# Local and global attention ahead of a gated feed-forward: the global queries of four heads put into one tile

## The chip, the cores and the metric

The program runs on one core of one Trainium2 chip. The metric is the device time of one execution in microseconds. For the kernel before the change three runs gave 1267.98, 1266.98 and 1265.59 us, so the median is 1266.98 us.

## What is computed

Each of 8 batches has 8 heads of dimension 64, with 512 local and 32 global tokens. A local query sees the 32 global keys and the local keys at most 32 positions away. A global query sees all 32 + 512 keys. The attention's result, 4608 tokens of 512 numbers, goes through a gated feed-forward with a hidden dimension of 1536.

```
s_g   = scale * q_g @ k_all.T           # 32 queries, 544 keys
out_g = sm(s_g) @ v_all
s_ll  = where(|i - j| <= 32, scale * q_l @ k_l.T, -1e9)
s_lg  = scale * q_l @ k_g.T
out_l = sm([s_lg, s_ll]) @ [v_g, v_l]
x     = [out_g, out_l]                  # per batch, heads side by side
y     = (sigmoid(x @ w_gate) * (x @ w_val)) @ w_out
```

The three weight matrices come as float64 and are turned into two float32r parts (high and low) on the chip; a product is then made of three matmuls, high x high, low x high and high x low.

## The kernel before

**The stream that sets the clock.** The feed-forward is one stream of TensorE matmuls (`ffn_stream`, L347). Its unit is an item: one chunk of tokens and one of 12 blocks of 128 hidden columns. An item has 12 matmuls into `bank_g`, 12 into `bank_v` (both L362) and 12 into `bank_o` (L396). After every four matmuls of 512 columns the generator yields. That is one tick, and a full chunk of 512 tokens has 9 x 12 = 108 ticks. The kernel keeps a list of events, each with a tick and an order; at every yield the driver issues the events that are due. So all work of the attention, of all engines, is written into the gaps between groups of feed-forward matmuls.

**Chunks.** Chunk 0 holds local blocks 0 and 1 of the first batch, chunk 1 its blocks 2 and 3 and its global queries, chunks 2 to 8 a batch each with its 32 global queries. The attention of chunk 0 runs ahead of the stream. The attention of chunk 1 and of chunk 2 runs during the feed-forward of chunks 0 and 1, while the weights are converted as well (`convert`, L119: four DVE operations, one ACT and one POOL operation for a block, three blocks every 4 ticks). From chunk 3 on the attention of one chunk runs in the 108 ticks of the chunk before it, the steady stage: six such periods of 8 heads. The last chunk and then the 256 global tokens of all batches go through the feed-forward with no attention beside them.

**Units of a head.** A head of a full chunk has two local units (two blocks of 128 queries each, `local_unit`, L216) and one global unit (32 queries, `global_unit`, L287). Each unit is a generator of four stages:

- local: (1) scores, four matmuls of 224 columns (L225), then mask and maximum on DVE (L237) and the exponential on ACT (L240); (2) normalisation on DVE (L243, L244 and L213); (3) four transposes of 128x128 on TensorE (L254), split into two float32r parts on ACT (L263) and DVE (L264); (4) four matmuls with the values (L280, L281), summed on ACT, DVE and POOL (L283 to L285).
- global: (1) four matmuls of 256 columns for the local keys (L299) and two of 32 columns for the global keys (L301), each into a PSUM bank of its own, then maxima on DVE (L304 to L306) and two exponentials on ACT (L308, L309); (2) normalisation of `pg`, 32 x 576, on DVE (L311, L312, L213); (3) five transposes of 32 rows (L317), split on ACT (L323) and DVE (L324); (4) five matmuls with the values (L330), summed on ACT, DVE and POOL (L335 to L337).

The heads of chunks 0 and 1 and the first four of chunk 2 use plain float32 ("native" in the code), the others the two float32r parts.

**What sets the order.** In the steady stage the units of a chunk follow each other every `PER` = 4 ticks and their stages lie at 0, 3, 6 and 9 ticks (`STAGES`), so a head takes 12 ticks and the TensorE work of scores, values and transposes falls into three different gaps of every four. `HOLE` puts all events of a chunk from its tick 8 on off by one tick. All PSUM tiles of the attention and `bank_g` and `bank_v` rotate through four buffers of one tag ("att"). The values of a head are in `vhl`, of which there are two buffers.

## Time and profile before

| | |
|---|---|
| median of three runs | 1266.98 us |
| the profiled execution: span from the first to the last instruction (the profile has no other time for it) | 1265.6 us |
| mean granted TensorE clock | 0.986 |
| TensorE matmul busy | 1221.5 us, 97%, 6820 instructions |
| DVE busy | 877.6 us, 69%, 2433 instructions |
| ACT busy | 783.3 us, 62%, 1899 instructions |
| POOL busy | 570.6 us, 45%, 573 instructions |
| bytes moved | 151.90 MB, mean 120 GB/s |
| start of the stream's first matmul | 49.71 us |
| a steady period (feed-forward of a chunk and attention of the next) | 139.1 us |
| the last chunk's feed-forward, with no attention beside it | 100.4 us |

How to read it: engine busy times are from the profile's first part; a busy TensorE is not one at its peak, since matmuls are pipelined and the duration of one includes the time to its last result. What a matmul costs the stream is therefore the distance from its start to the start of the next one, which the timeline gives.

### The profile page before, as it was taken

How to read it: one execution, taken by the hardware profiler on the slowest of the kernel's cores; microseconds unless marked ns; L12 is line 12 of the kernel's file. 1: busy time of each engine (PE TensorE's matmuls, PEld its weight loads, DVE VectorE, ACT ScalarE, POOL GpSimd, SP SyncE). 2: the span in 40 equal slices, each digit the busy share in tenths (PEclk: the TensorE clock that was granted, in tenths of full speed). 3: DMA queues.
4: the chain of work that ended last, by engine and by line, in shares of the span. 5: the costliest groups of instructions: out<-in, count | busy, mean ns of one | idle time of the engine just before them, and what ended most of it. 6: DMA issues, size and time to landing. Idle time of an engine off the chain costs nothing.

```text
span 1265.6 us, 20474 instructions
## 1 busy us (share of the span) xinstructions
PE 1221.5 (97%) x6820; PEld 994.1 (79%) x6820; DVE 877.6 (69%) x2433; ACT 783.3 (62%) x1899; POOL 570.6 (45%) x573
## 2 busy tenths in 40 slices
PE   5899989999999999999999999999999999999998
PEld 4676768788788877888788877888788877888897
DVE  4797976757877777857876778767775787632232
ACT  4586766756666666666666667756765766532233
POOL 1444554545555355545555455535554555311111
PEclk9698999999999999999999999999999999999999
DMA  5576864333333333333333423343334332122143
GB/s 198 197 259 225 254 191 145 92 121 99 92 107 98 115 99 108 91 121 108 107 92 107 126 78 107 109 127 111 92 86 126 116 92 87 44 90 67 67 133 117
DMA packets 59497, 151.90 MB, mean 120 GB/s; under 512 B 6144, under 2 KB 19456, under 8 KB 59392
## 3 DMA queue, kind: packets, MB, share of 16 engines
q1 hardware_dynamic: 59392, 150.59, 38.9%
q8 instruction: 54, 0.88, 0.3%
q14 instruction: 51, 0.42, 0.1%
HBM read 135.36 MB, written 15.20 MB: 119 GB/s over the span
## 4 chain that ended last, share of the span: by engine, by line
PE 77%; DVE 13%; ACT 5%; issue 3%; POOL 1%; DMA 1%; SPq 0%; POOLq 0%; DVEq 0%; ACTq 0%
PE bank_g L362 20%; PE bank_v L362 19%; PE bank_o L396 19%; PE bank_x L225 5%; PE bank_y L254 4%; DVE p_buf L213 3%; DVE th L378 2%; PE bank_y L317 2%; PE bank_x L330 2%; PE bank_x L280 2%; PE bank_x L299 2%; PE bank_x L281 1%; DVE pg_buf L213 1%; ACT s_sb L240 1%; DVE pt L264 1%
## 5 line engine op out<-in xcount | busy, mean ns | idle before, releaser
L362 PE MATMUL bank_g<-xt,wg 128*128 128x512 f32 (+1 forms) x1440 | 340.3, 371 | 1.8 <-DVE th L380 1.8
L362 PE MATMUL bank_v<-xt,wv 128*128 128x512 f32 (+1 forms) x1440 | 332.6, 368 | 3.0 <-DVE pt L264 2.7
L396 PE MATMUL bank_o<-wo,hh 128*128 128x512 f32 x1224 | 334.0, 404 | 0.8 <-ACT hh L382 0.4
L362 PEld LDWEIGHTS bank_g<-xt,wg 128*128 128x128 f32 x1440 | 238.6, 192 | 41.6 <-issue 3.4
L362 PEld LDWEIGHTS bank_v<-xt,wv 128*128 128x128 f32 x1440 | 237.8, 190 | 40.7 <-PE bank_y L301 3.1
L396 PEld LDWEIGHTS bank_o<-wo,hh 128*128 128x128 f32 x1224 | 214.1, 189 | 38.9 <-ACT hh L382 1.2
L383 POOL TENSOR_TENSOR hh<-th,hh 128x512 fp32r<-128x512 f32 (+1 forms) x120 | 137.6, 1147 | 199.7 <-ACT hh L382 198.8
L240 ACT ACTIVATE s_sb<-s_sb,nm 128x224 f32<-128x224 f32 x240 | 113.8, 475 | 143.1 <-DVE nm L237 142.0
L213 DVE TENSOR_SCALAR p_buf<-s_sb,r 128x128 f32<-128x128 f32 (+1 forms) x443 | 151.8, 386 | 4.2 <-PE bank_y L254 0.4
L375 DVE TENSOR_SCALAR mn<-bank_g 128x512 f32<-128x512 f32 (+1 forms) x108 | 67.3, 623 | 110.7 <-ACT th L370 109.3
L378 DVE SCALAR_TENSOR_TENSOR th<-th,mn 128x512 f32<-128x512 f32 (+1 forms) x120 | 101.5, 846 | 59.0 <-ACT mn L376 52.7
L285 POOL TENSOR_TENSOR x<-t 64x256 f32<-64x256 f32 x104 | 76.4, 734 | 142.8 <-DVE t L284 138.7
L194 POOL TENSOR_TENSOR kl<-qk_raw,qk_hi 128x704 fp32r<-128x704 f32 x52 | 88.4, 1701 | 114.8 <-ACT qk_hi L193 114.8
L370 ACT ACTIVATE th<-bank_g 128x512 f32<-128x512 f32 (+1 forms) x120 | 63.5, 529 | 97.7 <-PE bank_g L362 96.1
L382 ACT CAST hh<-th 128x512 fp32r<-128x512 f32 (+1 forms) x120 | 66.5, 554 | 68.1 <-DVE th L380 67.3
L237 DVE CUSTOM_DVE_ANT_0 s_sb<-bank_x,masks 128x224 f32<-128x224 f32 x240 | 83.8, 381 | 12.7 <-PE bank_x L225 8.4
L254 PE MATMUL bank_y<-ident,p_buf 128*128 128x128 f32 x496 | 80.1, 282 | 10.8 <-DVE p_buf L213 6.6
L196 POOL TENSOR_TENSOR qk_hi<-qk_raw,qk_hi 64x256 fp32r<-64x256 f32 x104 | 87.7, 863 | 4.1
L254 PEld LDWEIGHTS bank_y<-ident,p_buf 128*128 128x128 f32 x496 | 60.9, 143 | 32.5 <-ACT pg_buf L308 6.6
L243 DVE TENSOR_SCALAR r<-sm 128x2 f32<-128x2 f32 x128 | 29.3, 229 | 75.5 <-ACT s_sb L240 74.2
L193 ACT CAST qk_hi<-qk_raw 128x1248 fp32r<-128x1248 f32 x52 | 64.1, 1233 | 22.2 <-PE bank_y L301 22.1
L380 DVE TENSOR_TENSOR th<-bank_v,th 128x512 f32<-128x512 f32 (+1 forms) x120 | 72.4, 604 | 5.1 <-PE bank_v L362 1.3
(109 smaller groups left out, 1985.9 us busy)
## 6 DMA issues: line engine op xcount, KB each, us to landing
wo<-wo_dram SPq DMA_DIRECT2D x116, 512.0 KB, 3.5
qk_raw<-in_qk_dram SPq DMA_DIRECT2D x104, 312.0 KB, 4.4
v_raw<-in_v_dram SPq DMA_DIRECT2D x52, 256.0 KB, 2.6
out_dram<-ob SPq DMA_DIRECT2D x34, 256.0 KB, 3.0
xt<-in_w_gate_dram SPq DMA_DIRECT2D x12, 512.0 KB, 4.5
xt<-in_w_val_dram SPq DMA_DIRECT2D x12, 512.0 KB, 4.4
xt<-in_w_out_dram SPq DMA_DIRECT2D x12, 512.0 KB, 4.9
v_nat<-in_v_dram SPq DMA_DIRECT2D x8, 512.0 KB, 5.5
```

The source lines that it names most:

```text
L194: nc.gpsimd.tensor_tensor(kl, t[:, K0:Q1], hi[:, K0:Q1].bitcast(F32), op=ALU.subtract)
L196: nc.gpsimd.tensor_tensor(hi[64:128, r], t[64:128, r], hi[64:128, r].bitcast(F32), op=ALU.subtract)
L213: nc.vector.tensor_scalar(out, in_, by, None, op0=ALU.mult)
L237: anchor[0] = nc.vector.tensor_tensor_reduce(out=s_sb[:, i], in0=s_ps[:, i, 0:WIN], in1=masks[:, m], scale=-0.125, scalar=3.0e38, op0=ALU. ...
L240: nc.scalar.activation(s_sb[:, i], s_sb[:, i], AF.Exp, bias=nm[:, i:i + 1], scale=-1.0, accum_out=sm[:, i:i + 1])
L254: nc.tensor.transpose(pt_ps[:, 2 * i + t], pb[:, i, t * P:(t + 1) * P], ident)
L285: nc.gpsimd.tensor_tensor(dst, t0[:, :, 0], t0[:, :, 1], op=ALU.add)
L362: nc.tensor.matmul(acc, w[a][:, t, fs], xt[:, c, t, x0:x0 + ntok], start=n == 0, stop=n == 11)
L378: nc.vector.scalar_tensor_tensor(th, th, 1.0, mn, op0=ALU.add, op1=ALU.mult)
L380: nc.vector.tensor_tensor(th, acc, th, op=ALU.mult)
L383: nc.gpsimd.tensor_tensor(hh[:, 1, 0:ntok], th, hh[:, 0, 0:ntok].bitcast(F32), op=ALU.subtract)
L396: nc.tensor.matmul(o_ps[t], ph[:, a, t * P:(t + 1) * P], pwo[:, c], start=f2 == 0 and i == 0, stop=f2 == NF - 1 and i == 2)
```

## The change

The rows of four heads' global queries are collected in one tile of 128 partitions. `pg` grows from 32 to 128 partitions; head h writes its scores, unscaled, into partitions 32 (h mod 4) and up. Softmax, transposes and their split are then made once for four heads, by the last of them; the matmuls with the values are made for all four heads in one stage, 5 for each as before. The scores with the 32 global keys are no longer a matmul pair into a bank of their own: the second local unit of the head computes them ahead of its own scores, in columns 224 to 255 of the first block of its score bank, of which local scores use 224, and ACT copies them to `pg`. In `pg` these 32 keys now stand in columns 96 to 127, ahead of the 512 local ones, and the value rows on the host get a copy of the global values to match.

The schedule: a head takes `TICKS` = 12.25 ticks in place of 12, with its two local units 6.125 ticks apart (in place of 4, with the global unit in the third place). A local unit's transposes lie 6.125 ticks after its scores (in place of 6), which is the tick of the next unit's scores; at equal ticks the transposes come first. The global scores lie in the tick of the first unit's last stage, the other global stages 4, 6.75 and 11 ticks later. The first unit of a chunk starts at tick 1 in place of 3. For chunk 1 a head takes 2.2 ticks as before (one local unit, a global unit with offsets of its own), for chunk 2 it takes 9 as before; since the stages scale with the gap between local units, chunk 0's units (4 ticks apart as before) have stages at 0, 1.96, 4 and 5.88 ticks in place of 0, 3, 6 and 9.

Five value buffers in place of two, because the values of four heads are needed at once. `dynamic_dma_scratch_size=512` is passed to the program's constructor and frees the memory that they take.

```diff
-BASE, PER = 3, 4
-STAGES = (0, 3, 6, 9)
+GH = P // SG
+G0 = P - SG
+VBUFS = GH + 1
+BASE, TICKS = 1, 12.25
+LOCAL = ((0, 3), (3, 2), (TICKS / 2, 2), (9, 2))
+GLOBAL = ((9 - TICKS / 2, 3), (13 - TICKS / 2, 2), (15.75 - TICKS / 2, 2), (20 - TICKS / 2, 2))
+GLOBAL_HALF = ((2, 3), (4, 2), (6, 2), (10, 2))
-START = dict(per0=4, base1=1, per1=1.1, base2=23, per2=3, x2=28, lead=8, native_heads=4)
+START = dict(per0=4, base1=1, per1=2.2, base2=23, per2=9, x2=28, lead=8, native_heads=4)
...
-    pg = const.tile([32, 5 * P], F32, name="pg_buf")
+    pg = const.tile([P, 5 * P], F32, name="pg_buf")
...
         s_ps = ps.tile([P, 2, 256], F32, name="bank_x", tag="att", bufs=4)
+        with_gg = T["with_g"] and blocks[-1] == 3
+        if with_gg:
+            gg = s_ps[0:SG, 0, WIN:]
+            for t, (kt, k0) in enumerate(zip(ks, k0s)):
+                nc.tensor.matmul(gg, ks[0][:, QK - SG - q0:QK - q0], kt[:, k0 + 96:k0 + 128],
+                                 start=t == 0, stop=t == last)
...
+        if with_gg:
+            nc.scalar.copy(pg[SG * (h % GH):SG * (h % GH + 1), G0:P], gg)
         yield
...
-        for t, (src, k0) in enumerate(zip(ks, k0s)):
-            nc.tensor.matmul(sb, qg, src[:, k0 + 96:k0 + 128], start=t == 0, stop=t == last)
...
+        nc.scalar.copy(pg[SG * (h % GH):SG * (h % GH + 1), P:], sa)
+        if h % GH < GH - 1:
+            return
+        keys = pg[:, G0:]
+        nc.vector.tensor_reduce(mg[:, 0:1], keys, axis=AX.X, op=ALU.max)
+        nc.vector.tensor_scalar(mg[:, 0:1], mg[:, 0:1], -0.125, None, op0=ALU.mult)
+        nc.scalar.activation(keys, keys, AF.Exp, bias=mg[:, 0:1], scale=0.125, accum_out=sg)
         yield
+        nc.vector.tensor_scalar_add(mg[:, 1:2], sg, 1e-9)
+        nc.vector.reciprocal(mg[:, 1:2], mg[:, 1:2])
+        scaled(0, keys, keys, mg[:, 1:2])
         yield
+        for bank, c0, c1 in (("bank_x", 1, 5), ("bank_y", 0, 1)):
+            pt_ps = ps.tile([P, c1 - c0, P], F32, name=bank, tag="att", bufs=4)
+            for c in range(c0, c1):
+                nc.tensor.transpose(pt_ps[:, c - c0], pg[:, c * P:(c + 1) * P], ident)
+            nc.scalar.copy(pt[:, c0:c1, 0:P], pt_ps)
+            if not nat:
+                nc.vector.tensor_tensor(pt[:, c0:c1, P:], pt_ps, pt[:, c0:c1, 0:P].bitcast(F32), op=ALU.subtract)
         yield
+        o_ps = ps.tile([64, GH, 32] if nat else [P, GH, 2, 32], F32, name="bank_x", tag="att", bufs=4)
+        for g in range(GH):
+            vt = heads[h - GH + 1 + g]["v"]
+            for i, c in enumerate((1, 2, 3, 4, 0)):
+                p_c = pt[:, c].rearrange("p (a g q) -> p a g q", g=GH, q=SG)[:, :, g]
+                nc.tensor.matmul(o_ps[:, g], vt[:, (VS[3:] + VM)[c], :], p_c, start=i == 0, stop=i == 4)
...
-            for i in range(npu):
-                t0 = base + per * i
-                for o in STAGES:
-                    ev.append((t0 + sc * o, 2, lambda h=h, i=i: adv(h, i)))
+            for i in range(nu + with_g):
+                t0 = base + gap * min(i, nu - 1)
+                for o, order in (LOCAL if i < nu else GLOBAL if nu > 1 else GLOBAL_HALF):
+                    ev.append((t0 + sc * o, order, lambda h=h, i=i: adv(h, i)))
...
+        if j == 3:
+            ve[:, VS[j], G0:P] = vg
...
-    nc = bacc.Bacc("TRN2", target_bir_lowering=False, num_devices=1)
+    nc = bacc.Bacc("TRN2", target_bir_lowering=False, num_devices=1, dynamic_dma_scratch_size=512)
```

More of the change, by code (lines that the diff above doesn't have):

```diff
@@ L177, in load_v @@
             if T["h"] % ng == 0:
-                t = spl.tile([P, ng, nw, D], F32, name="v_nat", tag="vhl")
+                t = spl.tile([P, ng, nw, D], F32, name="v_nat", tag="vhl", bufs=VBUFS)
                 nc.sync.dma_start(t, v[n:n + ng, :, c].rearrange("n p j d -> p n j d"))
@@ L203, in split_v @@
         t = T["v_raw"]
-        vhl = spl.tile([P, 8, 2 * D], F32R, name="vhl")
+        vhl = spl.tile([P, 8, 2 * D], F32R, name="vhl", bufs=VBUFS)
         nc.scalar.copy(vhl[:, :, 0:D], t)
@@ L285, in local_unit, with global_unit @@
         nc.gpsimd.tensor_tensor(dst, t0[:, :, 0], t0[:, :, 1], op=ALU.add)
-    def global_unit(T, b, h):
+    def global_unit(T, b, h, heads):
         ks, k0s, q0 = T["qk"], T["k0"], T["q0"]
@@ L313, in global_unit @@
-        scaled(0, pg[:, 0:576], pg[:, 0:576], mg[:, 3:4])
+        nc.vector.tensor_scalar_add(mg[:, 1:2], sg, 1e-9)
+        nc.vector.reciprocal(mg[:, 1:2], mg[:, 1:2])
+        scaled(0, keys, keys, mg[:, 1:2])
         yield
-        pt_ps = ps.tile([P, 5, 32], F32, name="bank_y", tag="att", bufs=4)
-        for j in range(5):
-            nc.tensor.transpose(pt_ps[:, j], pg[:, j * P:(j + 1) * P], ident[0:32, 0:32])
-        if nat:
-            pt = att.tile([P, 5, 32], F32, name="ptg_nat", tag="ptg", bufs=1)
-            nc.scalar.copy(pt, pt_ps)
-        else:
-            pt = att.tile([P, 5, 64], F32R, name="ptg", bufs=1)
-            nc.scalar.copy(pt[:, :, 0:32], pt_ps)
-            nc.vector.tensor_tensor(pt[:, :, 32:64], pt_ps, pt[:, :, 0:32].bitcast(F32), op=ALU.subtract)
@@ L325, in global_unit @@
-        yield
-        vt = T["v"]
-        xg = xg32[prow:prow + 64, kt, b * SG:(b + 1) * SG]
-        o_ps = ps.tile([64, 32] if nat else [P, 64], F32, name="bank_x", tag="att", bufs=4)
-        for j in range(5):
-            nc.tensor.matmul(o_ps, vt[:, (VM + VS)[j], :], pt[:, j, :], start=j == 0, stop=j == 4)
-        if nat:
-            nc.scalar.copy(xg, o_ps)
+        pt = att.tile([P, 5, P if nat else 2 * P], F32 if nat else F32R, name="ptg", tag="ptg", bufs=1)
+        for bank, c0, c1 in (("bank_x", 1, 5), ("bank_y", 0, 1)):
[5 more added lines that the diff above has]
+                nc.vector.tensor_tensor(pt[:, c0:c1, P:], pt_ps, pt[:, c0:c1, 0:P].bitcast(F32), op=ALU.subtract)
@@ new lines, in global_unit @@
+        yield
+        o_ps = ps.tile([64, GH, 32] if nat else [P, GH, 2, 32], F32, name="bank_x", tag="att", bufs=4)
[4 more added lines that the diff above has]
+                nc.tensor.matmul(o_ps[:, g], vt[:, (VS[3:] + VM)[c], :], p_c, start=i == 0, stop=i == 4)
+        k0 = (h + 1 - GH) // 2
+        xg = [xg32[64 * i:64 * i + 64, k0:k0 + GH // 2, b * SG:(b + 1) * SG] for i in range(2)]
@@ L333, in global_unit @@
+        if nat:
+            for i in range(2):
+                nc.scalar.copy(xg[i], o_ps[:, i::2])
             return
-        y = att.tile([64, 64], F32, name="y", bufs=1)
+        y = att.tile([64, GH, 2, 32], F32, name="y", tag="t0", bufs=1)
         nc.scalar.copy(y, o_ps[64:128])
         nc.vector.tensor_tensor(y, o_ps[0:64], y, op=ALU.add)
-        nc.gpsimd.tensor_tensor(xg, y[:, 0:32], y[:, 32:64], op=ALU.add)
+        for i in range(2):
+            nc.gpsimd.tensor_tensor(xg[i], y[:, i::2, 0], y[:, i::2, 1], op=ALU.add)
@@ L407, in ffn_stream, with att_events @@
             prev = (C, f, hh, wo) if n_it < len(items) else None
-    def att_events(ci, start, per, tail=0):
+    def att_events(ci, start, period):
         b, blocks, with_g = chunks[ci]
@@ L427, in att_events @@
                 place = (raw, "qk_raw", QK)
-            heads.append(dict(first=ci == 0, native=native, h=h, n=b * NH + h, cols=slice(c0, c1),
+            heads.append(dict(first=ci == 0, with_g=with_g, native=native, h=h, n=b * NH + h, cols=slice(c0, c1),
                               wins=slice(0, 8 if with_g else 4), group=group, place=place))
@@ L433, in adv @@
                 gens[h, i] = (local_unit(heads[h], blocks[2 * i:2 * i + 2], x32s, h, 2 * i * P) if i < nu
-                              else global_unit(heads[h], b, h))
+                              else global_unit(heads[h], b, h, heads))
             next(gens[h, i], None)
-        npu = nu + (1 if with_g else 0)
+        gap = period / nu
+        sc = gap / (TICKS / 2)
         for h in range(NH):
             T = heads[h]
-            base = start + per * npu * h
-            sc = per / 4
+            base = start + period * h
             ev.append((base - sc * LOAD_QK, 0, lambda T=T: load_qk(T)))
@@ L482 @@
         t0 = 9 * NF * (ci - 2)
-        queue += [(t + width if t - t0 >= at else t, o, fn) for t, o, fn in att_events(ci, t0 + BASE, PER)]
+        queue += [(t + width if t - t0 >= at else t, o, fn) for t, o, fn in att_events(ci, t0 + BASE, TICKS)]
     for ci in range(2, G + 1):
@@ L500 @@
     queue.append((9 * NF * (G - 1) - 3, 9, split_globals))
-    queue.sort(key=lambda e: e[:2])
+    queue.sort(key=lambda e: (round(e[0], 6), e[1]))
     now = 0.0
```

16 lines of the change are left out of this document (3 added, 13 removed).

## The prediction

> **What bounds the kernel now.** First the page, for the share of each engine and the chain that ended last.
>
> ```profile
> span 1265.6 us, 20474 instructions
> ...
> PE 1221.5 (97%) x6820; PEld 994.1 (79%) x6820; DVE 877.6 (69%) x2433; ACT 783.3 (62%) x1899; POOL 570.6 (45%) x573
> ...
> PE 77%; DVE 13%; ACT 5%; issue 3%; POOL 1%; DMA 1%; SPq 0%; POOLq 0%; DVEq 0%; ACTq 0%
> ```
>
> TensorE (PE) is never long without work, and three quarters of the chain lie on it; DVE has 13%. An average hides stages with different limits, so next the busy time by stretches (length, then busy us of PE, PEld, DVE, ACT and POOL with instruction counts, granted clock, DMA share, GB/s).
>
> ```profile
> 45.00:75.00 30.00, 28.72 (x167) 22.14 (x166) 23.91 (x67) 20.79 (x61) 15.26 (x11) 0.82 0.71 242
> 75.00:105.00 30.00, 29.22 (x204) 21.75 (x203) 26.60 (x77) 24.14 (x77) 13.64 (x11) 1.00 0.80 255
> 105.00:135.00 30.00, 26.32 (x152) 20.82 (x152) 25.60 (x59) 18.67 (x54) 12.58 (x10) 0.83 0.69 215
> 135.00:165.00 30.00, 29.42 (x193) 23.03 (x192) 28.78 (x77) 23.43 (x68) 15.80 (x11) 1.00 0.82 263
> ...
> 410.00:549.10 139.10, 137.77 (x753) 112.17 (x753) 104.41 (x294) 92.35 (x214) 71.69 (x73) 1.00 0.36 106
> ```
>
> Two stages differ. From 45 to 165 us, where weights are converted, DVE is busy 104.9 of 120 us (87%) and the clock falls to 0.82 and 0.83 in two stretches: DVE is the limit, or close to it. A steady period (last row) has a full clock and DVE at 75%: there every TensorE matmul costs time. What it costs is read from the chain, which gives the pace of the stream, and the timeline, which gives the distances between starts.
>
> ```profile
> 549.13 2.88 PE bank_g L362 x12
> ...
> 688.31 2.88 PE bank_g L362 x12
> ...
> 1114.22 2.80 PE bank_g L362 x12
> 1117.02 2.80 PE bank_v L362 x12
> ```
>
> Twelve feed-forward matmuls of 512 columns take 1117.02 - 1114.22 = 2.80 us with nothing between them, 0.233 each. A period has 432 of them, 100.8 us, and takes 688.31 - 549.13 = 139.2. So the attention of 8 heads adds 38.4 us, 4.80 a head. Which group takes how much:
>
> ```profile
> 566.32 1.09 PE L396 MATMUL bank_o<-wo,hh 128*128 128x512 f32 x4
> 567.25 0.60 PE L254 MATMUL bank_y<-ident,p_buf 128*128 128x128 f32 x4
> 567.61 1.17 PE L396 MATMUL bank_o<-wo,hh 128*128 128x512 f32 x4
> 568.62 1.09 PE L362 MATMUL bank_g<-xt,wg 128*128 128x512 f32 x4
> ...
> 569.98 1.11 PE L362 MATMUL bank_g<-xt,wg 128*128 128x512 f32 x4
> 570.93 0.33 PE L280 MATMUL bank_x<-pt,vhl 128*128 128x256 f32 x1
> ...
> 571.45 1.10 PE L362 MATMUL bank_g<-xt,wg 128*128 128x512 f32 x4
> 572.47 0.49 PE L317 MATMUL bank_y<-ident,pg_buf 32*128 32x32 f32 x5
> 572.89 2.13 PE L362 MATMUL bank_v<-xt,wv 128*128 128x512 f32 x8
> 574.87 0.27 PE L225 MATMUL bank_x<-qk_hi 128*128 128x224 f32 x1
> ...
> 575.30 1.11 PE L362 MATMUL bank_v<-xt,wv 128*128 128x512 f32 x4
> 576.25 0.64 PE L330 MATMUL bank_x<-ptg,vhl 128*128 128x64 f32 x5
> 576.72 1.18 PE L396 MATMUL bank_o<-wo,hh 128*128 128x512 f32 x4
> 577.74 0.60 PE L254 MATMUL bank_y<-ident,p_buf 128*128 128x128 f32 x4
> ```
>
> Take the time from one feed-forward group to an event some groups later and subtract 0.233 for each feed-forward matmul between.
> - Local transposes (L254): 568.62 - 566.32 less 8 matmuls (1.87) is 0.43 for four, 0.108 each. The loss shows in two places: 0.36 until the next feed-forward matmul starts, and 0.08 behind it, in the group of four that runs 1.01 in place of 0.93.
> - Local scores (L225): 570.93 - 568.62 less 1.87 is 0.44 for four.
> - Global transposes (L317): 574.87 - 571.45 less 12 matmuls (2.80) is 0.62 for five, 0.124 each: more than a local one, though each has 32 rows and 32 columns.
> - Global values (L330): 577.74 - 575.30 less 1.87 is 0.57 for five.
>
> So a small matmul costs about 0.11 us whatever it computes.
>
> ```profile
> 580.02 0.28 PE L299 MATMUL bank_x<-qk_hi 128*32 128x256 f32 x1
> ...
> 580.50 0.18 PE L301 MATMUL bank_y<-qk_hi 128*32 128x32 f32 x1
> ...
> 580.56 1.18 PE L362 MATMUL bank_g<-xt,wg 128*128 128x512 f32 x4
> 581.57 0.28 PE L280 MATMUL bank_x<-pt,vhl 128*128 128x256 f32 x1
> ...
> 582.05 1.10 PE L362 MATMUL bank_g<-xt,wg 128*128 128x512 f32 x4
> ```
>
> Global scores take 580.56 - 580.02 = 0.54, 0.06 of it for the two with the global keys, and 0.08 behind them (581.57 - 580.56 is 1.01, not 0.93); local values 582.05 - 581.57 = 0.48. A head is then 2 x (0.44 + 0.43 + 0.48) + 0.62 + 0.62 + 0.57 = 4.51 of the 4.80 us. The other 0.29, 2.3 a period and 14 us over six, are waits of TensorE.
>
> **The change, part by part, on TensorE.**
>
> *Transposes.* Twenty of 32 rows become five of 128 rows for four heads. A new one is the shape of L254: 5 x 0.108 = 0.54 for four heads, 0.135 a head in place of 0.62. By L317's own 0.124 it is 0.155. I take 0.135: -0.485 a head.
>
> *Values.* Twenty matmuls of 64 columns for four heads before and after, in one gap in place of four: nothing; at most three exits of 0.08 go, 0.06 a head.
>
> *Global keys.* The same two matmuls, moved from the end of the global scores to the front of the local scores, where the weights change between 32 columns and 128 columns once more for each head. The trace has no such pair between two other small groups. Below, it costs nothing more (the 0.06 and an exit of 0.08 move along). Above, each of the two is exposed for its full 0.18, 0.36 - 0.06 = 0.30 more. I take +0.04, half an exit, since the same pair in the row above followed the 256-column matmuls without delay.
>
> *The shared gap.* Transposes and the next scores in one gap are the same eight matmuls at 0.11. At best the 0.08 behind the transposes is absorbed: 2 x 0.08 a head, 8 us over 48 heads; I take nothing. A head's ticks go from 12 to 12.25, but 8 x 12.25 = 98 of 108 ticks still hold it, and the stream, not the attention, sets the period.
>
> Steady sum: -0.485 + 0.04 = -0.445 a head, x 48 heads = **-21 us**.
>
> **On DVE**, by the rows of the groups:
>
> ```profile
> L264 DVE TENSOR_TENSOR pt<-bank_y,pt 128x512 fp32r<-128x512 f32 x104 | 70.1, 674 | 0.0
> ...
> L213 DVE TENSOR_SCALAR pg_buf<-pg_buf,mg 32x576 f32<-32x576 f32 x64 | 56.5, 883 | 1.9
> ...
> L304 DVE TENSOR_REDUCE mg<-bank_x 32x1 f32<-32x512 f32 x64 | 42.9, 671 | 7.4 <-PE bank_x L299 4.9 <-PE bank_y L301 2.4
> ...
> L324 DVE TENSOR_TENSOR ptg<-bank_y,ptg 128x160 fp32r<-128x160 f32 x52 | 15.9, 305 | 0.0
> ...
> L306 DVE TENSOR_SCALAR mg<-mg 32x1 f32<-32x1 f32 x64 | 12.8, 200 | 1.9
> ...
> L336 DVE TENSOR_TENSOR y<-bank_x,y 64x64 f32<-64x64 f32 x52 | 10.9, 209 | 18.6 <-ACT y L335 17.5
> ```
>
> A head now: 0.67 + 0.88 + 0.31 + 0.21, and four small ones of up to 0.2 (L306 is the longest), 0.7 together: 2.8 us. Four heads after: a reduce 0.67 and a scaling 0.88 (544 columns in place of 512 and 576; I take the number of partitions to cost nothing), subtractions 0.67 (L264's shape) and 0.31, three small ones 0.6, an addition of 256 columns between L336's 0.21 and 0.67, say 0.45: 3.6 us, 0.9 a head. DVE loses 1.9 us a head, 15 of its 104 us in a steady period. In exchange ACT copies scores twice a head, which its two exponentials for each head pay for. In the steady stage this work is off the path; it bears only on the 14 us of waits, and I leave those as they are: lighter DVE speaks for fewer, the batch in one burst (below) for more; +-8.
>
> In the startup it is on the path. The native heads have no subtraction and no addition, so they lose about 2.25 - 0.5 = 1.75 us of DVE: 14 us for the eight heads of chunk 1, and 4 for the two to three heads of chunk 2 before the conversions end (events until tick 45; heads from tick 23, every 9). DVE is not always the limit (87%), so I take two thirds of 18: **-12 us**, with 0 and -18 as bounds. The other five heads of chunk 2 gain as steady ones: 5 x 0.445, **-2 us**.
>
> *Before the stream.* Chunk 0's units lose overlap: by the event list the scores of unit k+1 now come behind the transposes of unit k; they were a unit ahead. The timeline shows that what is issued follows the list only loosely:
>
> ```profile
> 13.64 0.45 PE L254 MATMUL bank_y<-ident,p_buf 128*128 128x128 f32 x1 [2.67 <-DVE p_buf L213]
> 14.01 1.11 PE L225 MATMUL bank_x<-qk_nat 64*128 64x224 f32 x2
> 15.06 0.90 PE L254 MATMUL bank_y<-ident,p_buf 128*128 128x128 f32 x3
> ```
>
> Scores of a later unit lie between two transposes of the first one, so an order like this is filled where an operand is late. At worst each of seven units waits the 2.67 us of the first, 19 us; it can gain too where DVE no longer takes turns with two units. I take **+2**.
>
> *Queues, buffers and DMAs.* `gg`'s copy on ACT stands behind two exponentials and ahead of nothing that TensorE waits for within 6 ticks. `pg` is single: its next first write, by the fifth head's second unit (55.1 ticks after the first head's start), comes 2.6 ticks behind the transposes that read it (52.5). Loads keep their lead in ticks and their queue; three more value buffers take waits away. All at nothing; if a copy came late, the wait would stand at L317's successor.
>
> **Sum:** -21 - 12 - 2 + 2 = -33, against the profiled 1265.6: 1232.6. The median of the runs is 1.4 above that span: **1234 us**.
>
> **Rivals.**
>
> *Changing the array's shape costs more than the merged transposes bring in (12%).* For it: L317, whose weights have 32 rows, is dearer than L254 (0.124 against 0.108). Against it: 580.02 to 580.56. If the global pair ahead of the local scores is exposed in full, a head pays 0.30 more in place of my 0.04: 0.26 x 53 heads (48 and the five late ones of chunk 2) is 14 us, 1248. [...]
>
> *The waits go as well (14%).* With 15 us less of DVE in each period the 14 us vanish, 1220 or so. For it: the chain's 13% on DVE. Against it: the shared gap doubles what DVE and ACT get at once.
>
> *The burst (7%).* The last head of four issues its reduction of 544 columns ahead of the second local unit's normalisation (ticks 9 and 9.125 after the head's start), and the transposes of that unit are due three ticks later, at 12.25. DVE is in order: behind the reduction, which waits for ACT's copy of the scores, stand 0.67 + 0.2 and then two of 0.2 and four scalings. From the rows I make TensorE late by 0.2 to 0.7 us for a group, which is inside the waits above. If feed-forward work on DVE (0.7 to 1 us each) falls in between, it is more. There are 12 groups in the steady stage and 4 in the startup; from 33 / 16 = 2.1 us a group on, the change is slower; at 3 us it is 1281.
>
> *Nothing moves (3%).* The removed matmuls would have to lie where TensorE waits anyway. In the steady period it is busy 137.8 of 139.1, so they don't; only waits of equal size could bring this about.
>
> **How the numbers follow.** The forecast has 64%. Faster by over 0.2% (2.5 us, about what a measurement of this kernel can tell) holds it and the first two rivals, 90%; the same 3%; slower 7%. The range leaves out the burst, the null case and the far ends. Low: 1234 less some 17 (waits -8, startup -6, exits -3), 1217. High: 1234 plus 19 (the drain +14, chunk 0 +5), 1253.
>
> **What would show it.** L317's successor should have 80 transposes of 128x128, about 0.11 apart, and a steady period be 3.6 us shorter, 135.6. [...] DVE should be near 89 us in a period. The first stream matmul should start near 50 us and the stretch from there to chunk 2's first matmul be some 14 shorter. TensorE waiting on the local `p_buf` once in four heads by over 2 us would be the burst. A period longer than 137.5, or a startup that is not shorter, makes the forecast wrong.

## The result, and the profile after

Four runs of the changed kernel gave 1311.78 to 1317.1 us, median 1313.78, beside 1267.17 for the kernel before (1265.59 to 1267.98). The ratio is 1.037, with an interval of 1.035 to 1.0389: 47 us slower, where 33 us faster was forecast. The page of the profiled execution (1309.9 us, 44.3 more than before), its span, busy times and the chain's shares:

```profile
span 1309.9 us, 19366 instructions
...
PE 1217.6 (93%) x6580; PEld 996.5 (76%) x6580; DVE 766.9 (59%) x2064; ACT 763.5 (58%) x1726; POOL 560.7 (43%) x547
...
PE 47%; DVE 17%; ACT 14%; POOL 8%; DMA 7%; issue 6%; POOLq 0%; SPq 0%; DVEq 0%; ACTq 0%
```

Work went as planned: 240 TensorE matmuls and 111 us of DVE are gone. But TensorE's share of the chain fell from 77% to 47%, and ACT, POOL and DMA, 7% together before, now hold 29%. TensorE is no longer what everything else fits around; it waits.

Where the time came from, by the starts of the chunks' first `bank_g` matmuls (us):

| stretch | before | after | difference |
|---|---|---|---|
| up to the stream | 49.7 | 63.0 | +13.3 |
| stream start to chunk 2 | 222.4 | 216.6 | -5.8 |
| six periods | 833.5 | 867.9 | +34.4 |
| last chunk | 100.5 | 103.4 | +2.9 |
| the rest | 59.4 | 59.0 | -0.4 |

The last five of the six periods by stretches, before and then after (columns as in the prediction):

```profile
409.80:1105.60 695.80, 688.97 (x3762) 561.24 (x3762) 522.22 (x1470) 459.46 (x1070) 351.40 (x356) 1.00 0.35 102
```

```profile
421.10:1147.50 726.40, 682.21 (x3611) 563.74 (x3611) 448.42 (x1232) 445.21 (x961) 349.62 (x337) 0.99 0.34 98
...
672.60:690.00 17.40, 17.34 (x82) 14.41 (x83) 9.78 (x29) 10.88 (x23) 7.96 (x8) 0.84 0.30 83
```

Length less TensorE's busy time is TensorE's idle time: 6.8 us before, 44.2 after. That is more than the 30.6 by which the five periods grew, since busy time fell by 6.8. DVE lost 73.8, or 14.8 a period, as forecast (15), and nothing came of it. Who TensorE waits for is in the view of waits, over the same five periods (us in total, times, longest), before and after:

```profile
PE bank_x L280 <- DVE pt L264: 2.9, 7, 0.5
PE bank_v L362 <- DVE pt L264: 2.2, 5, 0.4
```

```profile
ACT vhl L215 <- DMA v_raw<-in_v_dram: 48.1, 19, 3.4
PE bank_x L316 <- ACT pg_buf L260: 14.6, 4, 3.7
PE bank_g L381 <- ACT xt L363: 7.2, 5, 1.7
PE bank_x L316 <- DVE mn L394: 6.8, 5, 2.1
PE bank_y L335 <- DVE mn L394: 6.2, 5, 1.2
PE bank_x L299 <- DVE pt L283: 4.2, 14, 0.5
```

The first row is not TensorE's, and before it didn't exist: ACT stands 48 us for loads of values. The timeline of ACT shows what that does (start, length, in brackets the idle time and who ended it):

```profile
666.18 0.62 ACT L215 CAST vhl<-v_raw 128x512 fp32r<-128x512 f32 x1 [2.74 <-DMA v_raw<-in_v_dram]
...
670.85 0.62 ACT L215 CAST vhl<-v_raw 128x512 fp32r<-128x512 f32 x1 [3.43 <-DMA v_raw<-in_v_dram]
671.37 0.48 ACT L257 ACTIVATE s_sb<-s_sb,nm 128x224 f32<-128x224 f32 x1
...
672.43 0.17 ACT L260 COPY pg_buf<-bank_x 32x32 f32<-32x32 f32 x1
```

Two casts, L215, issued ahead of work that is due sooner, hold ACT for 2.74 and 3.43 us until their loads land. Behind them on the same engine stand the exponentials of a local unit (L257), of which the first has its input from DVE by 668.44 and starts at 671.37, and the new copy `gg` (L260). Such casts come in groups of four: at 650.4, 656.1, 666.2 and 670.8 us, and then none before 720.3, where the kernel before starts one every 14 to 29 us. All loads go through one buffer, `v_raw`, so within a group each load starts only when the head before it has been cast (ACT) and subtracted (POOL): loads are issued at 661.46, 668.19 and 672.83 us, and POOL's subtractions end at 661.43, 668.16 and 672.80. TensorE at the same moment:

```profile
668.71 0.28 PE L300 MATMUL bank_x<-pt,vhl 128*128 128x256 f32 x1
672.66 0.42 PE L316 MATMUL bank_x<-qk_hi 128*32 128x256 f32 x1 [3.66 <-ACT pg_buf L260]
672.88 0.41 PE L316 MATMUL bank_x<-kl,qk_hi 128*32 128x256 f32 x1
...
673.51 3.61 PE L381 MATMUL bank_v<-xt,wv 128*128 128x512 f32 x8
676.93 1.63 PE L415 MATMUL bank_o<-wo,hh 128*128 128x512 f32 x4
```

The global scores (L316) need a PSUM buffer, and the next one in turn holds local scores which the copy has yet to read. TensorE waits 3.66 us, and afterwards works at half pace for a while: eight feed-forward matmuls take 676.93 - 673.51 = 3.42 us, 0.43 each in place of 0.233. The granted clock of the row from 672.60 on is 0.84, so some 2.8 of its 17.4 us go to that as well.

### The profile page after: what moved, and what is told of

Read it like the earlier page. It is cut to its first block, busy times and chain, and to the rows that moved or that the text cites. A ratio compares the mean times of both kernels' runs of the same rounds, so it can differ in the third digit from the quotient of the medians.

```text
span 1309.9 us, 19366 instructions
## 1 busy us (share of the span) xinstructions
PE 1217.6 (93%) x6580; PEld 996.5 (76%) x6580; DVE 766.9 (59%) x2064; ACT 763.5 (58%) x1726; POOL 560.7 (43%) x547
## 4 chain that ended last, share of the span: by engine, by line
PE 47%; DVE 17%; ACT 14%; POOL 8%; DMA 7%; issue 6%; POOLq 0%; SPq 0%; DVEq 0%; ACTq 0%
PE bank_g L381 12%; PE bank_o L415 12%; PE bank_v L381 12%; DMA v_raw<-in_v_dram 5%; ACT s_sb L257 4%; PE bank_x L242 3%; DVE p_buf L223 3%; PE bank_y L273 3%; POOL vhl L216 2%; DVE th L397 2%; PE bank_x L316 2%; POOL qk_hi L206 2%; DVE th L399 1%; POOL kl L204 1%; DVE pt L283 1%
## 5 line engine op out<-in xcount | busy, mean ns | idle before, releaser
L381 PE MATMUL bank_v<-xt,wv 128*128 128x512 f32 (+1 forms) x1440 | 329.1, 371 | 2.6 <-ACT pg_buf L260 2.6
L381 PE MATMUL bank_g<-xt,wg 128*128 128x512 f32 (+1 forms) x1440 | 318.3, 365 | 7.6 <-ACT xt L363 7.6
L415 PE MATMUL bank_o<-wo,hh 128*128 128x512 f32 x1224 | 317.0, 398 | 3.2 <-ACT hh L401 2.6
L381 PEld LDWEIGHTS bank_v<-xt,wv 128*128 128x128 f32 x1440 | 245.6, 194 | 47.7 <-ACT pg_buf L260 4.3
L415 PEld LDWEIGHTS bank_o<-wo,hh 128*128 128x128 f32 x1224 | 224.3, 190 | 50.4 <-ACT hh L401 4.0
L257 ACT ACTIVATE s_sb<-s_sb,nm 128x224 f32<-128x224 f32 x240 | 114.0, 475 | 108.2 <-DVE nm L254 107.3
L223 DVE TENSOR_SCALAR p_buf<-s_sb,r 128x128 f32<-128x128 f32 (+1 forms) x443 | 131.4, 354 | 3.7
L283 DVE TENSOR_TENSOR pt<-bank_y,pt 128x512 fp32r<-128x512 f32 x104 | 71.4, 687 | 99.2 <-ACT pt L282 99.1
L401 ACT CAST hh<-th 128x512 fp32r<-128x512 f32 (+1 forms) x120 | 66.6, 555 | 103.9 <-DVE th L399 103.5
L397 DVE SCALAR_TENSOR_TENSOR th<-th,mn 128x512 f32<-128x512 f32 (+1 forms) x120 | 93.4, 778 | 48.1 <-ACT mn L395 32.6
L262 DVE TENSOR_SCALAR r<-sm 128x2 f32<-128x2 f32 x128 | 37.8, 295 | 108.8 <-ACT s_sb L257 105.2
L216 POOL TENSOR_TENSOR vhl<-v_raw,vhl 128x512 fp32r<-128x512 f32 x52 | 67.0, 1288 | 74.7 <-ACT vhl L215 73.8
L204 POOL TENSOR_TENSOR kl<-qk_raw,qk_hi 128x704 fp32r<-128x704 f32 x52 | 88.7, 1705 | 20.9 <-ACT qk_hi L203 19.2
```

Source lines behind the costliest of these rows:

```text
L204: nc.gpsimd.tensor_tensor(kl, t[:, K0:Q1], hi[:, K0:Q1].bitcast(F32), op=ALU.subtract)
L216: nc.gpsimd.tensor_tensor(vhl[:, :, D:2 * D], t, vhl[:, :, 0:D].bitcast(F32), op=ALU.subtract)
L223: nc.vector.tensor_scalar(out, in_, by, None, op0=ALU.mult)
L257: nc.scalar.activation(s_sb[:, i], s_sb[:, i], AF.Exp, bias=nm[:, i:i + 1], scale=-1.0, accum_out=sm[:, i:i + 1])
L283: nc.vector.tensor_tensor(pt[:, 1], pt_ps, pt[:, 0].bitcast(F32), op=ALU.subtract)
L381: nc.tensor.matmul(acc, w[a][:, t, fs], xt[:, c, t, x0:x0 + ntok], start=n == 0, stop=n == 11)
```

## The experiments

The theory after this reading had three parts: (1) **the burst of casts**: with five value buffers and matmuls with the values once in four heads, four buffers come free at once, so four heads' loads and casts are issued in one go and ACT, which comes to the work behind a cast only after it (L257 above), stands for them; (2) **the new spacing** of the stages makes operands late, whether or not the tile is merged; (3) **chunk 0's stages**, closer together, cost the 13 us before the stream. Rivals: the buffers or the DMA memory as such; the merged tile itself (its array shape, its bursts on DVE). Times of a stretch below are of the profiled executions, ratios of the timed runs.

### e1_start: chunk 0's stages as before

```diff
-sc = gap / (TICKS / 2)
+sc = gap / 4 if ci == 0 else gap / (TICKS / 2)
+local = ((0, 2), (3, 2), (6, 2), (9, 2)) if ci == 0 else LOCAL
...
```

> The changed kernel with the stages of chunk 0 alone put back to 0, 3, 6 and 9 ticks (for units 4 ticks apart). Theory S: the 13.3 us by which the stream starts later (63.0 against 49.7 us) come from the order of chunk 0's units alone, one unit in flight in place of two; then the stream starts at about 50 us again and the time falls by 11 to 14 us, to 1300 to 1303. Rival: the later start comes from the loads (three value buffers more, loads in another order); then the stream still starts at 60 us or later and the time stays at 1311 to 1317.

1306.93 us, ratio 1.0302 (1.0262 to 1.0342). The stream starts at 48.4 us in place of 63.0, so chunk 0's stages do cause the late start. But chunk 2 is reached at 274.7 in place of 279.6: of 14.6 us only 4.9 are left. The row of stretches says why:

```profile
82.00:106.00 24.00, 24.00 (x107) 17.44 (x107) 13.12 (x33) 12.20 (x35) 5.80 (x5) 0.50 0.50 162
```

TensorE waits 2.0 us for `hh` at 80.96, and then has half a clock for 24 us without a gap, up to 12 us lost. The kernel after has the full clock there (1.00 from 80 to 120 us). That the wait is what takes the clock down is not shown: e12 has the same 24 us with no wait over 0.7 us ahead of them.

### e2_pin: the value cast held back

The cast is kept behind the exponential of the local scores that is written last ahead of it, so that it doesn't come early to ACT; the loads stay.

```diff
-nc.scalar.copy(vhl[:, :, 0:D], t)
+with tc.issue_after(act_anchor[0].ins):
+    nc.scalar.copy(vhl[:, :, 0:D], t)
...
-nc.scalar.activation(s_sb[:, i], ...
+act_anchor[0] = nc.scalar.activation(s_sb[:, i], ...
```

> The changed kernel with one edge more: ACT's cast of a head's values may not be issued ahead of the exponential that precedes it in the written order. Theory A (the values): with five buffers, four of them freed at once, the casts of four heads' values are issued together, far ahead; they share one load buffer, so ACT stands still for each load, with the local units behind it. Then the edge takes away ACT's waits for the value loads, a steady period falls from about 146 to 136 to 138 us, and the time by 45 to 60 us, to 1255 to 1270. Theory B (the burst on DVE and the shared gap cost the time, the casts only fill waits that are there anyway): a period stays above 143 and the time above 1295.

1285.88 us, ratio 1.0136 (1.0107 to 1.0166). The six periods take 840.6 us in place of 867.9: 27.3 us were the burst. The five periods, and TensorE's waits in them:

```profile
416.00:1120.70 704.70, 677.25 (x3612) 558.54 (x3611) 457.14 (x1231) 445.77 (x960) 349.07 (x336) 1.00 0.35 101
```

```profile
PE bank_g L383 <- ACT xt L365: 6.8, 5, 1.4
PE bank_y L337 <- DVE mn L396: 6.2, 5, 1.2
PE bank_x L301 <- DVE pt L285: 5.5, 14, 0.8
PE bank_y L275 <- DVE p_buf L225: 4.6, 10, 0.7
```

ACT's wait for `v_raw` and TensorE's for the copy at the global scores are gone, and so are 5.0 us of TensorE's busy time, for which the half pace can account. Idle time is 27.4 us, still 20.6 more than before. So the burst is a large part, not all.

### e3_before_bufs: the buffers alone

```diff
-vhl = spl.tile([P, 8, 2 * D], F32R, name="vhl")
+vhl = spl.tile([P, 8, 2 * D], F32R, name="vhl", bufs=5)
...
-nc = bacc.Bacc("TRN2", target_bir_lowering=False, num_devices=1)
+nc = bacc.Bacc("TRN2", target_bir_lowering=False, num_devices=1, dynamic_dma_scratch_size=512)
```

This is the kernel before with five value buffers.

> The kernel before with nothing but five value buffers in place of two and the smaller DMA scratch. Theory A with the release of four at once as its cause: here buffers come free one by one, casts stay one per head, and the time is that of the kernel before, 1264 to 1271. Rival A2 (depth alone: more buffers let loads and casts run ahead and ACT wait): ACT waits for value loads appear and the time rises by over 15 us. The scratch size costs nothing by either.

1266.55 us, ratio 0.9999 (0.9979 to 1.0019). Neither more buffers nor less DMA memory costs or brings anything: there a head's values are released one head at a time, and casts stay one a head. So it isn't the depth alone; what after and e6 have beside it is the release of four at once. Whether a second load buffer would take the waits away was not tried.

### e4_both: e1 and e2 together

> Both edits of the first two runs. By theories S and A together the losses add up: 1242 to 1257, below the kernel before. By S and B: about 1290 to 1303. By A and the rival of S: 1255 to 1270.

1282.34 us, ratio 1.0091 (1.0055 to 1.0128); ten runs spread from 1270.55 to 1287.69, more than any other kernel here. The profiled one, 1281.48 us, has 24 us of half clock in its startup as e1 has. By the mean granted clock on record, 0.985 in the three runs up to 1272.38 us and 0.976 to 0.979 in the four from 1280.5 to 1283.78, the shortest seem to lack that stretch (24 us at half clock is 0.009 of the mean); this is an estimate, for one run alone was profiled. Periods 840.9, stream start 47.6, chunk 2 at 275.6. The two repairs don't add up any better than e1 let expect: the start of the stream is 15 us earlier than in e2 and chunk 2 4.5 us. What is left of the change, the tile with its copies, the spacing of the stages and this stretch of the startup, still costs 0.9%; the next three take it apart.

### e5_oldstages_pin and e6_oldstages: the merged tile in the old spacing

e5 has the merged tile, the key pair in the local bank and five buffers, but the old 12 ticks a head with units every 4 ticks, and the cast held as in e2; e6 is e5 with the cast free. In chunk 1 of both, the fifth head's key pair is written into `pg` ahead of the first four heads' transposes, so that batch's global rows hold other numbers.

```diff
-BASE, TICKS = 1, 12.25
-LOCAL = ((0, 3), (3, 2), (TICKS / 2, 2), (9, 2))
...
+BASE, PER = 3, 4
+STAGES = (0, 3, 6, 9)
...
-START = dict(per0=4, base1=1, per1=2.2, base2=23, per2=9, x2=28, lead=8, native_heads=4)
+START = dict(per0=4, base1=1, per1=1.1, base2=23, per2=3, x2=28, lead=8, native_heads=4)
...
```

> The tile for four heads, the pair in the local score bank and the five buffers stay; the schedule is the old one (units every 4 ticks, stages at 0, 3, 6 and 9, the global unit in the third place, first tick 3), and ACT's value casts are held to their written place as in e2_pin. Theory D (what the casts leave over, 8 us of waits in a period, comes from the new spacing: transposes and scores in one gap, two PSUM tiles per gap, two or three ticks to the values): a period falls to 134 to 136.5 us and the time to 1235 to 1252, below the kernel before. Rival E (it comes from the batch itself, softmax and split of four heads in one burst): a period stays at 139 or above and the time at 1265 or above.

> As the run before, with the value casts free to run ahead. If the burst of casts costs what it cost in the changed kernel whatever the spacing, 5 us a period, the time is 28 to 35 us above the run before. If it only hurt together with the new spacing, the two are within 8 us.

e5: 1251.48 us, ratio 0.9881 (0.9849 to 0.9914), six periods 820.9, 12.6 us less than before. e6: 1269.88 us, 1.0023 (1.0012 to 1.0033), periods 841.8. The merged tile by itself is faster, so that rival falls; the burst alone takes that away, 20.9 us in the periods, by the same wait. (The profiled run of e6, 1273.62 us, is the longest of its eight; by the medians e6 is 18.4 us above e5.) Five periods of e6:

```profile
ACT vhl L212 <- DMA v_raw<-in_v_dram: 61.2, 29, 4.4
...
PE bank_x L296 <- DVE pt L280: 17.1, 16, 1.9
```

The same cause shows at another place: here TensorE is late by `pt`, whose first part ACT makes behind the casts.

### e7_sched_only: the new spacing alone

The kernel before, global units of one head as they were, with the new offsets (chunk 0's stages as before).

```diff
-BASE, PER = 3, 4
-STAGES = (0, 3, 6, 9)
+BASE, TICKS = 1, 12.25
+LOCAL = ((0, 3), (3, 2), (TICKS / 2, 2), (9, 2))
+GLOBAL = ((9 - TICKS / 2, 3), (13 - TICKS / 2, 2), (15.75 - TICKS / 2, 2), (20 - TICKS / 2, 2))
...
```

> The kernel before, each head's global unit by itself and its key pair in its own bank, with the new schedule alone (12.25 ticks a head, local units 6.125 apart, transposes in the gap of the next scores, first tick 1; chunk 0 keeps its old stages). Theory D: the spacing alone makes TensorE wait, a period rises from 139.1 to 143 to 147 us and the time to 1288 to 1318. Rival E: the spacing costs nothing by itself, 1262 to 1275.

1316.04 us, ratio 1.0401 (1.0362 to 1.044): alone it is as slow as the whole change. The periods take 858.9 us (25.4 more than before), the stretch to chunk 2 242.9 (20.5 more). The five periods and their largest waits:

```profile
431.90:1150.40 718.50, 692.26 (x3762) 567.70 (x3761) 491.57 (x1470) 452.51 (x1070) 355.05 (x357) 1.00 0.34 99
```

```profile
PE bank_y L303 <- DVE y L338: 8.1, 9, 1.2
PE bank_y L303 <- DVE mn L377: 5.8, 5, 1.2
PE bank_g L364 <- ACT xt L346: 4.8, 5, 1.0
PE bank_y L303 <- DVE th L382: 3.3, 5, 0.7
```

Idle time is 26.2 us, 19.4 more than before, with the full clock and no burst. L303, the global scores with the global keys, now follows local values and local-key scores in one gap and takes a third PSUM buffer in that gap; by the releasers (DVE's `y`, `mn` or `th`), the buffer's last reader isn't through yet. The first matmul of a chunk waits for `xt`, for the attention of the last heads ends later in a chunk. L303 holds 17.2 of the 26.2 us of idle time here, and the merged tile has no such matmul: there the new spacing costs 20.7 us over the six periods (e2 against e11), by other waits and in part as TensorE's busy time (677.25 against 670.96 us in five).

### e8_oldstages_pin2: e5 with chunk 1's key pair in place

Chunk 1's global stages start with the head, so that the pair of the fifth head no longer comes ahead of the four heads' transposes.

```diff
+HALF = (2.6, 5.2, 7.8, 13)
...
+half = i == nu == 1
+t0 = base if half else base + per * i
+for o in HALF if half else STAGES:
...
```

> As e5_oldstages_pin, whose chunk 1 wrote the fifth head's key pair into the shared tile ahead of the first four heads' transposes (so the global rows of that batch held other numbers); here chunk 1's global stages lie 0.7, 1.4, 2.1 and 3.6 ticks after the head's start, the transposes ahead of the next head's first stage. The tile for four heads is worth 21 us on TensorE in the steady stage and 2 to 6 us in the startup: 1240 to 1255, period 136.5 to 138. If the low time of e5_oldstages_pin hung on that order in chunk 1, 1258 or more.

1259.2 us, ratio 0.9941 (0.9923 to 0.9958): faster than before, but 7.7 us above e5. The periods are the same (820.1); the loss is in the startup, 231.9 us to chunk 2 in place of 218.3 (in its longest run, 1263.27 us; the median run, 4 us shorter, probably loses less). The waits from 82 to 114.6 us, and the stretches:

```profile
PE bank_x L335 <- DVE pg_buf L223: 3.4, 1, 3.4
```

```profile
82.00:87.00 5.00, 1.56 (x11) 0.98 (x10) 3.84 (x11) 2.94 (x8) 1.79 (x2) 1.00 0.70 252
87.00:104.00 17.00, 17.00 (x84) 12.76 (x83) 8.66 (x25) 8.51 (x26) 6.11 (x6) 0.50 0.54 175
104.00:115.00 11.00, 11.00 (x62) 7.50 (x61) 4.81 (x15) 9.06 (x25) 4.13 (x5) 0.99 0.59 190
```

One wait of 3.4 us for the normalised tile, and then 17 us at half clock in which TensorE has no gap at all.

### e9_g1_later: the global scores in a gap of their own

e4 with the global scores 10.5 ticks after the head's start in place of 9, out of the gap of the first unit's values. The theory on trial was that this shared gap holds most of the 20 us that the spacing costs.

```diff
-GLOBAL = ((9 - TICKS / 2, 3), ...
+GLOBAL = ((10.5 - TICKS / 2, 3), ...
```

> The kernel of e4_both (new spacing, casts held, chunk 0 as before) with the global scores 1.5 ticks later, so that they no longer share a gap with a local unit's values. Theory P (waits for one of the four rotating PSUM tiles are what the new spacing adds, above all where values and global scores want two or three tiles in one gap): a period falls from 141.2 to 137.5 to 139.5 us and the time by 10 to 22. Rival L (the shorter way from a unit's transposes to its values and the later end of the attention cost it): 140.3 or more.

1283.89 us, ratio 1.0152 (1.0118 to 1.0186); periods 846.9, 6.0 more than e4. The wait at the shared gap went, and another grew:

```profile
PE bank_g L383 <- ACT xt L365: 15.1, 5, 3.0
PE bank_y L337 <- DVE mn L396: 5.0, 5, 1.0
```

At 1.5 ticks later the last heads' attention ends later still, and each chunk's first matmul waits 3.0 us for `xt` (1.4 in e2). The theory falls as a net gain: waits only moved. Over five periods TensorE's idle time is that of e4 (28.3 and 28.0 us); what is longer is its busy time (684.8 and 677.0 us), at a granted clock of 0.99 in place of 1.00.

### e10_chunk1: chunk 1's old, closer stages in the new spacing

```diff
-sc = gap / 4 if ci == 0 else gap / (TICKS / 2)
+sc = gap / 4 if ci == 0 else gap / 8 if ci == 1 else gap / (TICKS / 2)
-local = ((0, 2), (3, 2), (6, 2), (9, 2)) if ci == 0 else LOCAL
+local = ((0, 2), (3, 2), (6, 2), (9, 2)) if ci < 2 else LOCAL
...
-GLOBAL_HALF = ((2, 3), (4, 2), (6, 2), (10, 2))
+GLOBAL_HALF = ((2.6, 2), (5.2, 2), (7.8, 2), (13, 2))
```

The rest is e4; the question was whether the spread of chunk 1's stages lengthens the startup.

> The kernel of e4_both with the old, closer stages in chunk 1 (0.275 ticks per step in place of 0.359, scores in gaps of their own). Theory C1 (chunk 1's new spacing is what makes the stretch from the first stream matmul to chunk 2 228 us long, against 218 in e5_oldstages_pin): the stretch falls to 216 to 222 and the time by 6 to 12. Rival C2 (it is chunk 2's spacing, or the clock of that execution): 225 or more.

1287.58 us, ratio 1.0162 (1.0145 to 1.0178). The stretch to chunk 2 is 233.7 us, not shorter than e4's 228.0: that theory falls too. The same wait of 3.4 us as in e8 stands in it, with the same half clock behind it.

### e11_delay: e8 with room for the normalisation

Chunk 1's heads 4 to 7 are put off by 1.5 ticks and the global stages spread, so that the transposes come when the tile is ready.

```diff
-HALF = (2.6, 5.2, 7.8, 13)
+HALF = (2.6, 8, 13, 18.2)
...
-base = start + per * npu * h
+base = start + per * npu * h + (1.5 if ci == 1 and h >= GH else 0)
```

> As e8_oldstages_pin2, with chunk 1's heads 4 to 7 put off by 1.5 ticks, so that the batch of the first four has 2.9 ticks in place of 1.4 from its scores to its transposes. Theory T (in chunk 1 TensorE comes to the batch's transposes before their normalisation is done, waits 3.4 us, and runs the next 30 us with a clock of 0.74): the stretch from the first stream matmul to chunk 2 falls from 232 to 216 to 223 us and the time to 1242 to 1251. Rival: the stretch stays at 228 or above, and the low time of e5_oldstages_pin had another cause.

**1248.08 us, ratio 0.9859 (0.9839 to 0.9879)**: the fastest of all, 19 us under the kernel before. The wait of 3.4 us is gone, the same stretch has the full clock, and chunk 2 comes 218.6 us after the stream's start (231.9 in e8):

```profile
87.00:104.00 17.00, 16.17 (x114) 12.00 (x113) 13.80 (x40) 15.66 (x46) 7.79 (x6) 1.00 0.76 226
400.80:1085.70 684.90, 670.96 (x3613) 553.01 (x3612) 464.39 (x1230) 446.34 (x959) 341.62 (x335) 1.00 0.36 104
```

In the same 17 us TensorE starts 114 matmuls in place of 84. The second row has the merged tile's true price in the steady stage: over five periods 18.0 us less of TensorE's busy time than before, 3.6 a period, and 13.9 us idle, 7.1 more.

### e12_ticks12: the new spacing with 12 ticks a head

e4 with `TICKS` = 12 in place of 12.25. The theory: the attention of the last heads ends too late for the next chunk's `xt`, and that is a good part of what the spacing costs.

```diff
-BASE, TICKS = 1, 12.25
+BASE, TICKS = 1, 12
```

> The kernel of e4_both (new spacing, casts held, chunk 0 as before) with 12 ticks a head in place of 12.25: local units 6 apart, every step of a local unit three ticks, the attention of a chunk done two ticks earlier. Theory L (the quarter tick costs it: some units get two ticks from transposes to values, and the last heads' tokens come late for the next chunk's first matmuls): a period falls from 141.2 to 136 to 138.5 us, the time to 1252 to 1268. Rival P (sharing gaps, with two PSUM tiles at once, costs it at any period): 139.5 or more, 1272 or more.

1268.32 us, ratio 1.0007 (0.9995 to 1.0018). The periods are 824.6 us, 16.3 less than e4's 840.9: 12.25 ticks cost 2.7 us a period. Five periods of e12:

```profile
PE bank_x L301 <- DVE pt L285: 9.5, 14, 1.0
PE bank_v L383 <- DVE t L305: 5.6, 5, 1.1
PE bank_x L318 <- ACT pg_buf L262: 3.2, 5, 0.7
```

No wait for `xt` is left, nor the one for `mn` at the second tile of transposes. Some 0.8 us a period remain against the old spacing (819.9 in e11). Most of the rest of its distance to e11 is startup: 231.5 us to chunk 2, with the half clock of e1 (0.57, 0.50 and 0.74 in the three stretches of ten us from 80 on, by which it is 0.50 from about 81.4 to 105), here with no wait over 0.7 us in the ten us ahead of it.

### What the six periods add up to

| kernel | merged tile | spacing | casts | six periods, us |
|---|---|---|---|---|
| before | no | old | free | 833.5 |
| e7 | no | new | free | 858.9 |
| e11 (e5, e8) | yes | old | held | 819.9 (820.9, 820.1) |
| e6 | yes | old | free | 841.8 |
| e2 (e4) | yes | new | held | 840.6 (840.9) |
| e12 | yes | new, 12 ticks | held | 824.6 |
| after | yes | new | free | 867.9 |

From before by e11 and e2 to after: -13.6 for the merged tile, +20.7 for the spacing, +27.3 for the burst, together the +34.4 of the result. Each term was also measured in another setting: the spacing +25.4 (e7 against before, by other waits) and +26.1 (after against e6), the burst +20.9 (e6 against e5). The last chunk's +2.9 goes with the spacing as well: 103.9 us in e2, 100.5 in e11.

## Why the prediction was wrong, step by step

- **"Loads keep their lead in ticks and their queue; three more value buffers take waits away. All at nothing."** This step failed most: +27.3 us in the periods. Leads in ticks say when a load may be issued at the earliest; what spaced the loads was the release of two buffers, one head at a time. With the release in fours, casts come to ACT ahead of work due sooner and wait there: 19 times in five periods, for 1.1 to 3.4 us each. The prediction asked what stands behind `gg`'s copy on ACT, not what now stands ahead of it.
- **"In the steady stage this work is off the path; it bears only on the 14 us of waits, and I leave those as they are"**, and **"8 x 12.25 = 98 of 108 ticks still hold it"**: failed, +20.7 us. The ticks hold the work's issue, but it ends too late for `xt`, which the next chunk's first matmuls read (6.8 us in e2, gone in e12): of the 20.7 us 12.25 ticks cost 16 (e12). The shared gaps were priced by their matmuls alone, without the operands and PSUM buffers that come late for them (in e2 6.2 us at the second tile of the global transposes, 5.5 at the values). That it is a PSUM buffer is inferred from the releasers. e9 shows that such a stall can be moved but not so simply removed.
- **"Chunk 0: +2"**, with 19 as the worst: +13.3. The way it goes is the one described as the worst; the timeline of before has two units in flight, and from 24.6 to 35.3 us a faster pace:

```profile
27.36 0.30 PE L254 MATMUL bank_y<-ident,p_first 128*128 128x128 f32 x1 [0.50 <-DVE p_first L213]
27.59 0.64 PE L225 MATMUL bank_x<-qk_nat 64*128 64x224 f32 x2
```

  In the timeline of after one unit is in flight, TensorE waits for it each time, and the pace doesn't rise (a pair of scores takes 1.11 us, not 0.64):

```profile
31.75 0.45 PE L273 MATMUL bank_y<-ident,p_first 128*128 128x128 f32 x1 [1.52 <-DVE p_first L223]
32.13 1.11 PE L242 MATMUL bank_x<-qk_nat 64*128 64x224 f32 x2
```

  Not all of it is the order. e6, with the old stages of chunk 0, doesn't reach the faster pace ahead of its stream either and starts it at 52.96 us; the other kernels with the old stages start it at 47.2 to 49.7. By that comparison some 10 of the 13.3 us are the order, and the rest the pace.

- **"Two thirds of 18: -12 us"** and -2 more in the startup: -5.8 after, -3.8 in e11. DVE's busy time in the whole stretch fell from 178.0 to 157.1 us; the 18 were reckoned for its part until the conversions end. So the saving on DVE came, and less than a third of it reached the end: 87% busy as DVE was, most of what it lost was off the path, or other waits took its place. Which of the two is not taken apart.
- **The transposes, values, key pair:** right. In e11's timeline five transposes take 532.50 - 532.03 = 0.47 us and 0.04 behind them, 0.51 for the 0.54 forecast, and the 20 matmuls with the values 537.48 - 535.34 = 2.14 in one gap, where four groups of 0.57 took 2.28. In after's timeline:

```profile
446.05 0.60 PE L273 MATMUL bank_y<-ident,p_buf 128*128 128x128 f32 x4
...
446.93 2.97 PE L381 MATMUL bank_g<-xt,wg 128*128 128x512 f32 x12
...
453.01 0.60 PE L273 MATMUL bank_y<-ident,p_buf 128*128 128x128 f32 x4
453.36 0.26 PE L236 MATMUL bank_x<-qk_hi 128*32 128x32 f32 x1
...
454.03 2.92 PE L415 MATMUL bank_o<-wo,hh 128*128 128x512 f32 x12
456.78 0.28 PE L299 MATMUL bank_x<-pt,vhl 128*128 128x256 f32 x1
...
457.25 0.28 PE L316 MATMUL bank_x<-qk_hi 128*32 128x256 f32 x1
...
457.72 2.97 PE L381 MATMUL bank_g<-xt,wg 128*128 128x512 f32 x12
```

  Transposes and scores in one gap take 446.93 - 446.05 = 0.88 without the key pair and 454.03 - 453.01 = 1.02 with it: the pair costs 0.14 a head, and the global scores now 457.72 - 457.25 = 0.47 in place of 0.62, 0.01 less in sum (forecast +0.04). So the rival of the costlier array shape didn't happen: with the change from 32 to 128 columns in it the pair costs this 0.14 and no more. The 14 us that the range's upper end has for "the drain" is a term that no run shows; in its place the runs show 0.14 for the pair and 0.47 for the scores. The prediction's "a small matmul costs about 0.11 us whatever it computes" doesn't fit this pair: two of 32 columns took 0.06 before and 0.14 now. By TensorE's busy time the merged tile brings 3.6 us a period (e11), the 3.56 that 8 x 0.445 gives; 1.4 us of it are lost again to waits, above all for `pt` (11.8 us in its five periods). What is left over six periods is the 13.6 of the forecast 21.
- **The rivals.** The only slower one was a burst on DVE, behind the reduction of 544 columns. A burst it was, but of casts on ACT. TensorE waits for the local `p_buf` only 4.6 us in five periods of e2, 0.7 at the longest, inside the 0.2 to 0.7 of the prediction. That DVE comes to its work in order, as that rival has it, shows in after: idle for 3.29 us until the split (L283) at 667.45, it reads the scores behind it, done at 664.79, only from 668.06. That DVE's and the gap's reliefs would take waits away (14%) was the reverse of what came; nor were there 14 us to take, for that was the rest of the prediction's sum, and TensorE's idle time was 6.8 us in five periods. "A period longer than 137.5" was named as what would show the forecast to be wrong; the five periods of after take 145.3 us each.

What stays open: which of the PSUM rotation and the later operands makes the last 0.8 us a period of the new spacing, what takes the clock down in the startup of e1, e4, e9 and e12, and why three of e4's runs take 1287 us at a mean clock of 0.985. None of these was tried.

## What to carry to other kernels

A step that takes its inputs for several heads at once releases their buffers at once, and every prefetch that was paced by those buffers can then come in a burst, as the casts here did (48.1 us of ACT's waits in five periods, none before): list, for each buffer whose release moves, what is issued on its release and which engine will stand for it, with the work behind it. A gain read off the bottleneck engine (here 3.6 us a period of TensorE's busy time, as computed) reached the end only with the order of the work as it was, so try the merge in the old schedule before the schedule in the new one. And behind a wait of TensorE of some us read the granted clock: the 3.4 us of e8 were followed by 17 us at half clock, 8.5 us of lost pace.
